# Weight chunks issued ahead of all crossbar transposes, with unit order and due times from a search

## Chip, cores, metric

The kernel runs on one core of one Trainium2 chip. The metric is the device time of one execution in microseconds (us), lower is better. In the text PE is TensorE, DVE is VectorE, ACT is ScalarE, POOL is GpSimd and SP is SyncE, as the profile calls them; "L456" is line 456 of the kernel of that run, so the same statement has different line numbers in different kernels.

## The reference

Attention with hard routing, then an MLP with exact gelu. Shapes: q, k, v are (4, 8, 768, 64), so 32 heads; 16 centroids per head; the MLP takes 3072 tokens from 512 to 2048 and back to 512.

```python
q_assign = np.argmax(np.einsum('bhsd,hcd->bhsc', q_n, c_n), axis=-1)   # q_n, k_n, c_n: normalized
k_assign = np.argmax(np.einsum('bhsd,hcd->bhsc', k_n, c_n), axis=-1)
mask = q_assign[:, :, :, None] == k_assign[:, :, None, :]
scores = np.where(mask, scale * np.matmul(q, k.transpose(0, 1, 3, 2)), -1000000000.0)
attn = softmax(scores)                       # [...] written out in the reference
x = (attn @ v).transpose(0, 2, 1, 3).reshape(B * S, H * D)
h = x @ w_in
out = (0.5 * h * (1.0 + erf(h / np.sqrt(2)))) @ w_out
```

## The kernel before

The kernel is written as a list of operations (`Op`), each with an engine, an estimated duration, dependences, and a due time. At build time a list scheduler (`Plan.run`) plays a small timing model and fixes the order in which each engine gets its instructions: it takes for each engine the operation that can start first, and among those that can start together the one with the smallest due time. The chip then runs that order, and waits where the model was wrong. A dependence that is added to this list by hand only changes the order: the chip gets no wait for it.

```python
    def run(self):
        # [...]
                    key = (t, op.due)              # t: earliest start in the model
                    if first is None or key < first:
                        first, pick = key, op
        # [...]
            dur = op.dur
        # [...]
            if op.dma:
                q = "POOL" if e == "POOL" else "SP"
                other = "SP" if q == "POOL" else "POOL"
                at = max(dma_free[q], t + 0.8)
                dma_free[q] = at + op.dma * (1.8 if dma_free[other] > at else 1.0)
                op.end = max(t + dur, dma_free[q] + 1.6) + (0.8 if t > 6 else 0.0)
```

One head goes through these steps. SP loads k, q, v (192 KB each). POOL splits k and q into a high and a low fp16 half, tile `st` (for the first three heads ACT makes the high halves). The halves are transposed into `kqT`: on PE for heads 0 to 7, by a crossbar transpose on SP for heads 8 to 31. PE then multiplies with the centroids (`asn_ps`), DVE makes one-hot rows, and these are appended to `kqT` so that the score matmul applies the mask. ACT takes the exponential of the scores (`p_sb`), PE multiplies with v (`x_ps`), DVE normalizes (`x_tok`). When 8 heads are done, PE turns the tokens (`fin_ps`, copied to `xt`) and the MLP of that batch starts: `hp`, gelu, then the second product `op`, done with seven half-size products in place of eight, for which DVE forms 16 sums of weight blocks once.

```python
            def dtr():
                nc.sync.dma_start_transpose(
                    out=new_T().rearrange("p a n d -> p (a n) d"),
                    in_=T["st", i].rearrange("p a n d -> p (a n) d"))   # heads 8 to 31
            e = add("SP", 1.4, due - 10, dtr, [sp["k"], sp["q"]], take=[s_T], dma=2.2, name=f"dtr{i}")

    def weight(n, due, deps=()):                 # 8 chunks, cast to fp16 on the way, issued by POOL
        # [...]
        w_ops[n] = add("POOL", 0.8, due,
                       lambda: nc.gpsimd.dma_start(out=dst, in_=src), deps, dma=3.6, name=f"w{n}")

    W_AT = (2, 3, 4, 5, 7, 8, 9, 10)
    # [...]
    for n in range(8):
        weight(n, need[n + 3] - 16, [splits[W_AT[n]]["k"]])   # chunk n after the split of head W_AT[n]

    def make_weight_sums(due):                   # 16 sums on DVE, 128x512 fp16 each
        for n in range(4):
            fs = slice(2 * n, 2 * n + 2)
            wd = [w_ops[4 + n // 2], w_ops[6 + n // 2]]
            o3 = add("DVE", 0.33, due, lambda fs=fs: sub(t3[:, fs], b22[:, fs], b12[:, fs]), wd, name=f"t3_{n}")
            # [...] t1, t2, t4 likewise

    # order of work: u = half a head of attention, f = half a batch of the first MLP product
    seq = [("u", *u) for u in ((0, 0), (0, 1), (1, 0), (1, 1), (2, 0), (3, 0), (2, 1), (4, 0), (5, 0), (3, 1),
        (6, 0), (7, 0), (4, 1), (5, 1))]
    seq += [("f", 0), ("u", 6, 1), ("u", 7, 1), ("u", 8, 0), ("u", 8, 1), ("f", 1)]
    # [...]
```

The softmax here doesn't subtract the row's maximum and nothing guards it: scores larger than these inputs give would overflow.

Of the kernel before, what the change touches and what calls it, by code (L numbers as in the profile page):

```python
# [15 lines left out]
BIG = 30.0  # L16

LATENCY = {"PE": 0.22, "ACT": 0.12, "DVE": 0.12, "POOL": 0.15, "SP": 0.1}

# [10 lines left out]
class Slot:  # L30


    def __init__(self, pool):
        self.pool, self.users, self.place = pool, [], None


class Plan:



    def __init__(self, pools, filler, filler_until):
        self.ops, self.pools = [], pools
        self.taken = {p: [] for p in pools}
        self.filler, self.filler_until = filler, filler_until

    def add(self, *a, **k):
        op = Op(*a, **k)
        self.ops.append(op)
        return op

    def free_at(self, slot):

        taken, bufs = self.taken[slot.pool], self.pools[slot.pool]
        if len(taken) < bufs:
            return 0.0
        last = 0.0
        for u in taken[len(taken) - bufs].users:
            if u.end is None:
                return None
            last = max(last, u.end)  # L60
        return last

    def run(self):
# [11 lines left out]
        while n:  # L75
# [35 lines left out]
            op.start = t  # L111
            dur = op.dur
            if op.func is not None and op.func != func:
# [11 lines left out]
            for s in op.take:  # L125
                self.taken[s.pool].append(s)
            done.append(op)
# [10 lines left out]
def kernel(  # L138
# [40 lines left out]
    for n in ("sc", "m", "x", "opX", "opY"):  # L179
# [25 lines left out]

    plan = Plan(POOLS, lambda: nc.tensor.matmul(warm_ps[:, 0:QB], dm[:, 0:128],
                                                dm[:, 128:128 + QB],
# [4 lines left out]
    def copy(eng, o, i):  # L212
# [5 lines left out]

    seq = [("u", *u) for u in (
        (0, 0), (0, 1), (1, 0), (1, 1), (2, 0), (3, 0), (2, 1), (4, 0), (5, 0), (3, 1),  # L220
        (6, 0), (7, 0), (4, 1), (5, 1))]
    seq += [("f", 0), ("u", 6, 1), ("u", 7, 1), ("u", 8, 0), ("u", 8, 1), ("f", 1)]
    for i in range(9, NH):
        if i % H == 1:
            seq += [("u", i, 0), ("f", 2 * (i // H) - 2), ("f", 2 * (i // H) - 1),
                    ("u", i, 1)] if i > H + 1 else [("u", i, 0), ("u", i, 1)]
        else:
            seq += [("u", i, 0), ("u", i, 1)]
    seq += [("f", 2 * B - 2), ("f", 2 * B - 1)]
    pos, at = {}, 0  # L230
# [32 lines left out]
    def memsets3():  # L263
# [10 lines left out]
        accum_out=cent_ssq), [ld_cent], name="ssq")  # L274
    c3 = add("POOL", 0.25, -79, lambda: nc.gpsimd.tensor_tensor(
        cent_norm, cent_ssq, half, op=ALU.pow), [c1, o_dm], name="root")
# [40 lines left out]
    OH_DMA = 8  # L317
    W_AT = (2, 3, 4, 5, 7, 8, 9, 10)
    ACC = set(range(0, 8))
# [4 lines left out]
    def make_load(i):  # L324
# [14 lines left out]
        loads[i] = dict(zip("kqv", ops))  # L339
        return slots  # L340

    def make_split(i, slots):
# [7 lines left out]
        for n, w in enumerate("kq"):  # L350
            def hi(w=w, n=n):
                if ("st", i) not in T:
                    T["st", i] = pool["st"].tile([128, 2, N, 2 * D], FP16, tag="st",
                                                 name="st")
                t = T[w + "st", i] = T["st", i][:, n]
                copy(eng_hi[w], t[:, :, 0:D], T[w + "raw", i])

            def lo(w=w):
                t = T[w + "st", i]
                engine[eng_lo[w]].tensor_sub(t[:, :, D:2 * D], T[w + "raw", i],  # L360
                                             t[:, :, 0:D])
            a = add(eng_hi[w], DUR[eng_hi[w]][0], due + n, hi, [ld[w]]
                    + ([hi_k] if w == "q" else []), take=[s_st] if w == "k" else [],
                    name=f"hi{w}{i}")
            hi_k = a
            c = add(eng_lo[w], DUR[eng_lo[w]][1], due + n + 0.5, lo, [a],
                    name=f"lo{w}{i}")
            res[w] = c
            slots["qkv".index(w)].users = [a, c]
        s_va = Slot("va")  # L370

        def vcast():
            nc.gpsimd.tensor_copy(vaugs[i % POOLS["va"]][:, :, 0:D], T["vraw", i])  # L373
        vc = add("POOL", 0.52, first[i] - (4 if i == 0 else 12), vcast, [ld["v"], o_va],
# [4 lines left out]

    early_ohs = {}  # L380

    def make_prep(i):
# [46 lines left out]
        else:  # L429
            def dtr():  # L430
# [4 lines left out]
                    name=f"dtr{i}")  # L435
            sp["st"].users = [e]
            ready["k"] = ready["q"] = e
        s_m = Slot("m")
# [52 lines left out]
        def ge():  # L491
            o = oh_solo[i] if solo else ohs[(i // 2) % POOLS["oh"]][:, :, i % 2]
            nc.vector.tensor_tensor(o[:, :, :, 0:C], src(),
                                    T["amax", i].to_broadcast([128, N, 2, C]),
                                    op=ALU.is_ge)
        d = 0.36 if acc else 0.28
        m1 = add("DVE", d, due + 5, amax, deps, take=[s_am], name=f"amax{i}")
        m2 = add("DVE", d, due + 5.2, ge, [m1, o_oz],
                 take=[s_oh] if s_oh is not None and i % 2 == 0 else [], name=f"ge{i}")
        if acc:  # L500
# [13 lines left out]
    def make_oh(heads):  # L514
# [7 lines left out]
        def oh(j):  # L522
            if solo:
                return oh_solo[i0][:, j].rearrange("p a b -> p (a b)")
            return ohs[(i0 // 2) % POOLS["oh"]][:, j].rearrange("p a b c -> p (a b c)")

# [7 lines left out]
        def ohdma():  # L534
            t = pool["ohT"].tile([128, N, 128], FP16, tag="ohT", name="ohT")
            nc.sync.dma_start_transpose(
                out=t, in_=ohs[(i0 // 2) % POOLS["oh"]].rearrange("p n a b c -> p (n a b c)"))
            T["ohps", i0] = t.rearrange("p n d -> p (n d)")
# [9 lines left out]
        for e, i in enumerate(heads):  # L548
# [15 lines left out]
            d = [tr, *asn_ops]  # L564
            dur = 0.35 if by_dma else 0.56
            pk = add(eng, dur if eng == "DVE" else 0.8, need[i] - 3,
# [15 lines left out]
    for n in range(8):  # L582
        weight(n, need[n + 3] - 16, [splits[W_AT[n]]["k"]])

# [4 lines left out]
    xtok_slot = {b: Slot("xtok") for b in range(B)}  # L589
    fin_ops, fin_seen = {}, set()  # L590

# [3 lines left out]
    def make_unit(i, t):  # L595
# [41 lines left out]
        for jj in range(NJ):  # L637
            def av(jj=jj):
# [5 lines left out]
                for ch in range(N):  # L644
                    nc.tensor.matmul(o, T["p", i, t][:, ch, jj * 128:(jj + 1) * 128],  # L645
                                     vaugs[i % POOLS["va"]][:, ch, 0:D + 1],
                                     start=(ch == 0), stop=(ch == N - 1))
# [19 lines left out]
        def nrm():  # L667
            if ("xtok", b) not in T:
# [5 lines left out]
                T["rec", key].to_broadcast([128, nn, D]), op=ALU.mult)  # L674
        r = add("DVE", 0.19, p0 + 5.5, rec, src, take=[Slot("rec")], name=f"rec{key}")
        m = add("DVE", 0.56 if nn == N else 0.36, p0 + 5.6, nrm, [r],
                take=[xtok_slot[b]] if ("n", b) not in norm_ops else [],
                name=f"norm{key}")
        r.take[0].users = [m]
# [10 lines left out]
    def make_fin(b, m, t, due):  # L690
        tt = (t,) if b == 0 else (0, 1)
        deps = [norm_ops[b * H + 2 * m, t], norm_ops[b * H + 2 * m + 1, t]]
        take = [] if b in fin_seen else [xt_slot[b]]
        fin_seen.add(b)
        js = slice(NJ * t, NJ * (t + 1)) if b == 0 else slice(0, N)
# [18 lines left out]
        def fin():  # L714
# [6 lines left out]
        e = add("DVE", 0.36 if nj < N else 0.56, due + 0.3, lambda: nc.vector.tensor_copy(  # L721
            xt(), T["fin", b, m, t][:, 0:nj * 128]), [f], take=take, name=f"fev{b}{m}{t}")
        s_m.users = [e]
# [58 lines left out]
    def make_weight_sums(due):  # L782
        for n in range(4):
            fs = slice(2 * n, 2 * n + 2)
            wd = [w_ops[4 + n // 2], w_ops[6 + n // 2]]
            o3 = add("DVE", 0.33, due, lambda fs=fs: sub(t3[:, fs], b22[:, fs], b12[:, fs]),
                     wd, name=f"t3_{n}")
            o1 = add("DVE", 0.33, due, lambda fs=fs: sub(t1[:, fs], b12[:, fs], b11[:, fs]),
                     [o3], name=f"t1_{n}")
            o2 = add("DVE", 0.33, due, lambda fs=fs: sub(t2[:, fs], b22[:, fs], t1[:, fs]),  # L790
                     [o1], name=f"t2_{n}")
            o4 = add("DVE", 0.33, due, lambda fs=fs: sub(t4n[:, fs], b21[:, fs], t2[:, fs]),
                     [o2], name=f"t4_{n}")
# [3 lines left out]
    def make_fc2(b, lo, hi):  # L797
# [6 lines left out]
        for n in range(NB // 2):  # L804
# [3 lines left out]
            def sums(k_, fs=fs):  # L808
# [7 lines left out]
                else:  # L816
                    sub(*{2: (s2, s1, a11), 3: (a21, a11, a21), 4: (a12, a12, s2)}[k_])
            ga, gb = gel_a[2 * n:2 * n + 2], gel_b[2 * n:2 * n + 2]
            o1 = add("DVE", 0.48, due, lambda f=sums: f(1), gb,
                     take=[s_S] if n == 0 else [], name=f"S1_{b}{n}")  # L820
            o2 = add("DVE", 0.48, due, lambda f=sums: f(2), [o1, *ga], name=f"S2_{b}{n}")
            o3 = add("DVE", 0.48, due, lambda f=sums: f(3), [o1, *ga], name=f"S3_{b}{n}")
            o4 = add("DVE", 0.48, lo + 0.46 * (hi - lo), lambda f=sums: f(4), [o2],
                     name=f"S4_{b}{n}")
# [27 lines left out]

        def result(name, j, emit, deps, due, eng="DVE", keep=None, bank=None, dur=0.36):
            take = []
# [20 lines left out]
        for k_, (p, j, xy) in enumerate(turns):  # L875
# [65 lines left out]
            if ("u3", j) in sums_out and ("p5", j) in sums_out and \  # L941
# [3 lines left out]
                    [sums_out["u3", j], sums_out["p5", j]], due + step, eng="POOL",  # L945
                    keep="o", dur=0.65)
                slots["u3", j].users.append(o)
# [50 lines left out]
```

## Time and profile before

The kernel before took 319.6 us (median of 3, 318.75 to 321.26). In the profiled execution, by engine busy time:

| | PE | ACT | DVE | POOL |
|---|---|---|---|---|
| busy, us of 319.0 | 292.8 | 217.6 | 182.5 | 118.6 |

PE is the bottleneck on average (a busy PE need not be at its peak: its matmuls overlap, so that six `hp` matmuls of 0.33 us take 1.14 us together). The average hides a hole. The next lines are from the page's view of the span in 40 slices of 8 us; a digit is tenths of the slice that PE was busy, and tenths of full clock that PE was granted:

```profile
PE   6899951799998998999999999999999999899995
PEclk9999995789999999999999999999999999999999
```

Read the sixth slice on (40 to 64 us): PE is at 5, 1 and 7 tenths, and the clock at 5 and 7 tenths follows right behind. The waits of PE, summed by what it waited for (total, times, longest, in us), name the cause:

```profile
PE asn_ps L456 <- DMA kqT<-st: 11.3, 2, 9.4
PE sc_ps L608 <- DVE kqT L560: 1.8, 4, 0.7
```

Two waits for a crossbar transpose cost 11.3 us; nothing else is over 2 us. Busy time by stretch (window, length, then busy us and instructions of each engine, then the clock, the mean number the page calls DMA share, and GB/s):

```profile
core 0: us, PE busy (x) PEld busy (x) DVE busy (x) ACT busy (x) POOL busy (x), PEclk, DMA share, GB/s
30.00:40.00 10.00, 9.53 (x180) 7.37 (x178) 8.39 (x23) 9.10 (x13) 9.75 (x16) 1.00 1.13 266
45.50:54.80 9.30, 0.00 (x0) 0.00 (x0) 0.54 (x2) 0.83 (x2) 0.00 (x0) 0.70 1.34 146
54.80:65.00 10.20, 8.21 (x87) 5.31 (x88) 4.91 (x12) 5.93 (x7) 5.54 (x9) 0.67 1.23 201
```

From 45.5 to 54.8 us PE does nothing and the other engines nearly nothing: the whole core waits for a transfer. Then PE works at about two thirds of its clock for 10 us. The transfers in question, first the two transposes by their SP instructions, then the four chunks of `w_out` by their POOL instructions (durations are min/median/max in ns):

```profile
L431 SPq DMA_TRANSPOSE kqT<-st x2: 7188/8985/10782, 36.1 to 44.6; - x2
...
  PE asn_ps L456: 11.3, 2
DMA to landing us min/median/max: 17.8/18.3/18.7
...
L312 POOL DMA_DIRECT2D w_out_sb<-in_moe_w_out_dram x4: 747/778/787, 29.0 to 41.5; - x4
DMA to landing us min/median/max: 11.9/18.7/20.7
```

The transposes of heads 8 and 9, issued at 36.1 and 44.6 us, take 18.7 and 17.8 us to land, and SP itself is held 7.2 and 10.8 us by issuing them (median of all 24: 1.6). All 24 transposes have a median of 4.7 us to land. Three weight chunks, issued at 36.2, 37.0 and 41.5 us, are in flight at the same time and take 18 to 21 us.

### The profile page before, as it was taken

Reading aid. Unit: us, or ns where it says so; the run is one execution under the profiler, and the core shown is the slowest. Engines: PE = TensorE matmul, PEld = TensorE weight load, DVE = VectorE, ACT = ScalarE, POOL = GpSimd, SP = SyncE. Lnnn points to the kernel's source line nnn. Section 1 sums busy time; section 2 is a strip of 40 time slices with the busy share of each in tenths; the row PEclk is TensorE's granted clock in tenths of the full one; section 3 lists DMA queues with packets and bytes.
Section 4 is the critical chain, followed back from the end, with each engine's and each line's share of the span. In section 5 each row is a group of like instructions: output and inputs, shape, how many; then the busy total and the mean of one; then the engine's idle time right before and its main releaser. Section 6 shows DMA issues by size and latency. Waiting matters only on the chain.

```text
span 319.0 us, 8302 instructions
## 1 busy us (share of the span) xinstructions
PE 292.8 (92%) x3392; PEld 213.9 (67%) x3392; DVE 182.5 (57%) x432; ACT 217.6 (68%) x278; POOL 118.6 (37%) x192
## 2 busy tenths in 40 slices
PE   6899951799998998999999999999999999899995
PEld 3587730467765886766667887876678887666784
DVE  4578840499689559475155558574364573203663
ACT  5487970747967887798668888896678878566200
POOL 5999921473462365566200574640000010000020
PEclk9999995789999999999999999999999999999999
DMA  7899999995982899999403799871006132100112
GB/s 265 263 246 254 257 89 162 182 243 164 174 218 65 125 194 197 253 224 238 109 0 73 176 227 181 133 153 30 2 0 111 56 78 61 51 2 0 35 66 99
DMA packets 78038, 43.50 MB, mean 136 GB/s; under 512 B 57008, under 2 KB 77488, under 8 KB 78000
## 3 DMA queue, kind: packets, MB, share of 16 engines
q1 hardware_dynamic: 75024, 38.55, 56.9%
q0 software_dynamic: 2688, 4.19, 8.5%
q8 instruction: 26, 0.43, 0.5%
q10 hardware_dynamic: 288, 0.23, 0.2%
q14 instruction: 12, 0.10, 0.1%
HBM read 27.30 MB, written 6.29 MB: 105 GB/s over the span
## 4 chain that ended last, share of the span: by engine, by line
PE 74%; DMA 12%; DVE 6%; POOL 3%; issue 2%; ACT 2%; SPq 0%; POOLq 0%; DVEq 0%
PE hp L747 26%; PE op L889 20%; PE sc_ps L608 14%; DMA kqT<-st 10%; PE x_ps L645 9%; PE asn_ps L456 2%; DVE kqT L557 2%; POOL st L360 1%; ACT p_sb L617 1%; DMA ohT<-oh 1%; PE tr_ps L412 1%; DMA v_raw<-in_v_dram 1%; DVE kqT L560 1%; DVE S L815 1%; POOL st L216 1%
## 5 line engine op out<-in xcount | busy, mean ns | idle before, releaser
L617 ACT ACTIVATE p_sb<-sc_ps 128x768 f16<-128x768 f32 x192 | 147.8, 809 | 36.9 <-PE sc_ps L608 34.5
L608 PE MATMUL sc_ps<-kqT 80*128 80x384 f16 x384 | 94.5, 329 | 2.3 <-DVE kqT L560 1.8
L747 PE MATMUL hp<-xt,w_in_sb 128*128 128x384 f16 x512 | 88.0, 329 | 0.3 <-DVE xt L721 0.2
L761 ACT ACTIVATE g<-hp 128x768 f16<-128x768 f32 x64 | 51.8, 810 | 36.3 <-PE hp L747 36.3
L747 PEld LDWEIGHTS <-w_in_sb 128*128 128x128 f16 x512 | 49.5, 99 | 32.6 <-issue 2.2
L645 PEld LDWEIGHTS <-p_sb 128*128 128x128 f16 x1152 | 57.4, 98 | 20.6 <-PE sc_ps L608 1.9
L645 PE MATMUL x_ps<-vaug,p_sb 128*128 128x65 f16 x1152 | 64.7, 195 | 1.8 <-DVE x_tok L672 1.1
L889 PEld LDWEIGHTS <-g 128*128 128x128 f16 x480 | 44.9, 97 | 10.4 <-issue 1.0
L943 POOL TENSOR_TENSOR c<-u,p 128x256 f32<-128x256 f32 x12 | 9.2, 768 | 114.5 <-DVE p L927 80.9
L889 PE MATMUL op<-w_out_sb,g 128*128 128x256 f16 x288 | 38.9, 272 | 0.2 <-DVE p L910 0.2
L608 PEld LDWEIGHTS <-kqT 80*128 80x128 f16 x384 | 29.7, 99 | 6.6 <-DVE kqT L560 2.6
L373 POOL CAST vaug<-v_raw 128x384 f16<-128x384 f32 x32 | 16.9, 530 | 43.1 <-PE x_ps L645 41.2
L360 POOL TENSOR_TENSOR st<-k_raw,st 128x384 f16<-128x384 f32 x31 | 28.7, 926 | 2.6 <-ACT st L214 0.4
L360 POOL TENSOR_TENSOR st<-q_raw,st 128x384 f16<-128x384 f32 x31 | 28.3, 919 | 1.7
L815 DVE TENSOR_TENSOR S<-g 128x768 f16<-128x768 f16 x16 | 9.5, 594 | 31.7 <-ACT g L761 31.6
L216 POOL CAST st<-k_raw 128x384 f16<-128x384 f32 x29 | 15.0, 520 | 33.6 <-DMA kqT<-st 33.6
L889 PE MATMUL op<-w_st,g 128*128 128x256 f16 x192 | 27.1, 272 | 0.4 <-DVE u L922 0.3
L472 DVE TENSOR_REDUCE asb<-asn_ps 128x192 f32<-128x384 f32 x24 | 13.3, 553 | 17.6 <-PE asn_ps L456 17.3
L456 PE MATMUL asn_ps<-c_cat,kqT 128*128 128x32 f16 x288 | 11.4, 177 | 11.3 <-DMA kqT<-st 11.3
L889 PEld LDWEIGHTS <-S 128*128 128x128 f16 x192 | 17.9, 97 | 5.5 <-DVE S L779 1.8
L672 DVE TENSOR_TENSOR x_tok<-x_ps,rec 128x384 f16<-128x384 f32 (+1 forms) x40 | 19.1, 477 | 1.3
L456 PEld LDWEIGHTS <-kqT 128*128 128x128 f16 x288 | 10.4, 96 | 13.5 <-DMA kqT<-st 11.8
(81 smaller groups left out, 276.5 us busy)
## 6 DMA issues: line engine op xcount, KB each, us to landing
q_raw<-in_q_dram SPq DMA_DIRECT2D x32, 192.0 KB, 3.4
v_raw<-in_v_dram SPq DMA_DIRECT2D x32, 192.0 KB, 4.0
out_dram<-c SPq DMA_DIRECT2D x48, 128.0 KB, 2.0
k_raw<-in_k_dram SPq DMA_DIRECT2D x31, 192.0 KB, 3.5
w_in_sb<-in_moe_w_in_dram POOLq DMA_DIRECT2D x4, 512.0 KB, 7.7
w_out_sb<-in_moe_w_out_dram POOLq DMA_DIRECT2D x4, 512.0 KB, 18.7
kqT<-st SPq DMA_TRANSPOSE x24, 4.7
k_raw<-in_k_dram ACTq DMA_DIRECT2D x1, 192.0 KB, 3.6
```

Of the source, the lines that this page charges most:

```text
L216: engine[eng].tensor_copy(o, i)
L360: engine[eng_lo[w]].tensor_sub(t[:, :, D:2 * D], T[w + "raw", i], t[:, :, 0:D])
L373: nc.gpsimd.tensor_copy(vaugs[i % POOLS["va"]][:, :, 0:D], T["vraw", i])
L456: nc.tensor.matmul(o, t[:, js], c_cat[:, h].rearrange("p a c -> p (a c)"), start=True, stop=True)
L472: nc.vector.tensor_reduce(out=T["asb", i], in_=T["asn", i].rearrange("p n w (a c) -> p n w c a", a=2), axis=AX.X, op=ALU.add)
L608: nc.tensor.matmul(s_ps[:, e, 0:QB], T["kT", i][0:D + C, c * 128:(c + 1) * 128], T["qT", i][0:D + C, t * QB:(t + 1) * QB], start=True, sto ...
L617: nc.scalar.activation(T["p", i, t][:, 2 * cp:2 * cp + 2, :], T["sc", i, t, cp][:, :, 0:QB], ACT_FN.Exp, bias=0.0, scale=float(scale))
L645: nc.tensor.matmul(o, T["p", i, t][:, ch, jj * 128:(jj + 1) * 128], vaugs[i % POOLS["va"]][:, ch, 0:D + 1], start=(ch == 0), stop=(ch == N ...
L672: nc.vector.tensor_tensor(T["xtok", b][:, h // 2, j0:j0 + nn, h % 2 * D:(h % 2 + 1) * D], T["x", key][:, :, 0:D], T["rec", key].to_broadca ...
L747: nc.tensor.matmul(T["hp", hb, fp][:, e, 0:QB], w_in_sb[:, m, f * 128:(f + 1) * 128], T["xt", b][:, m, t * QB:(t + 1) * QB], start=(m == 0 ...
L761: nc.scalar.activation(T["g", hb][:, :, fp, :], T["hp", hb, fp][:, :, 0:QB], ACT_FN.Gelu, bias=0.0, scale=1.0)
L889: nc.tensor.matmul(T["op", b, key], a()[:, f, j * 128:(j + 1) * 128], w[:, f, :], start=(start and f == 0), stop=(f == NB - 1), skip_group ...
```

## The change

The intent: issue the weight chunks earlier, so that all of them have landed before the first crossbar transpose; hold the splits and transposes of heads 8 and later behind the last chunk in the plan; correct the durations of the timing model; and search, on that model, over the order of the units and over a shift of the due time of single operations. No arithmetic is added or removed. Buffers that were picked by head number are picked in the order of emission, so that the new order stays correct.

```diff
+ORDER = ("0a 0b 1a 1b 2a 3a 4a 5a 2b 6a 7a 4b 5b 3b f0 6b 7b 8a 8b f1 9a 9b [...] f6 f7 ")
+SHIFT = dict(... "fc2_2_P6_0_1=41 fc2_0_P1_1_1=20 [... about 1,600 entries ...] av14a1=-5")
     def add(self, *a, **k):
         op = Op(*a, **k)
+        op.due += self.shift.get(op.name, 0)
-            dur = op.dur
+            dur = op.dur + (0.03 if e == "DVE" else 0.0)
-    W_AT = (2, 3, 4, 5, 7, 8, 9, 10)
+    W_AT = (1, 2, 3, 4, 5, 6, 7, 7)
-        weight(n, need[n + 3] - 16, [splits[W_AT[n]]["k"]])
+        weight(n, need[W_AT[n]] - 14, [splits[W_AT[n]]["kq"[n == 7]]])
+    for i in range(8, NH):
+        if i not in PE_TR:
+            first_hi[i].deps.append(w_ops[7])      # first split of head i
+            dtrs[i].deps.append(w_ops[7])          # its crossbar transpose
-            o3 = add("DVE", 0.33, due, ...         # the 16 weight sums
+            o3 = add("DVE", 0.69, due, ...
-                nc.gpsimd.tensor_copy(vaugs[i % POOLS["va"]][:, :, 0:D], T["vraw", i])
+                nc.gpsimd.tensor_copy(vaugs[turn("va", i)][:, :, 0:D], T["vraw", i])
[... other durations (S sums 0.48 to 0.58, results 0.36 to 0.41), the same for the one-hot buffers ...]
```

`ORDER` is nearly the old order: half a head is moved here and there. Most of the search's result is in `SHIFT`.

The two dependences on `w_ops[7]` are called the explicit waits below.

## The prediction

> **What bounds it now.** TensorE: 292.8 of 319.0 us busy. But busy is not peak: from the trace's start-to-start times (0.16 us per 384-column matmul, 0.11 per 256, 0.03 per 65) I estimate only about 250 us of matmul work. In stretches (busy time by window), the lost time sits in three places:
> - 45.5 to 54.8 us: TensorE does nothing. The waits view gives 9.4 us to the first crossbar transpose of an attention head (kqT from st, head 8), and 2.0 us to the next, ending at 62.5. Both together are 10% of the chain of waits. The granted clock is 0.50 from 50 to 58 and 0.60 from 62 to 66, which I estimate at 3 us more. [...]
> - 100 to 147 us: TensorE 43.3 of 47 us, ScalarE 39.7. Neither is saturated; the chain goes through a one-hot transpose (4.2 us), a kqT transpose (5.4), POOL splits.
> - 147 to 213.6: 66.6 us for one steady batch; the next batch takes 62.7. ScalarE's own work there (48 exps, 16 gelus paced by TensorE, 2 table loads) is about 61.
>
> **Why the transposes stall.** The first transposes start at 36.1 and 44.6 us and take 18.7 and 17.8 us to land (median of all 24: 4.7). Three weight chunks, issued by POOL at 36.2, 37.0 and 41.5, are in flight and take 18 to 21 us (the first ones took 7 to 10). SP is itself held 7.2 and 10.8 us by the two transpose issues (1.3 to 1.6 normally), and POOL idles 12.6 us for a st buffer. [...]
>
> **What changes.** No arithmetic is added or removed. Instruction order shows weights issued earlier in POOL's stream, and heads 8 and later split and transposed only after the last chunk has landed. Adding up POOL's durations, the last three chunks move from 36.2/37.0/41.5 to about 31/32/33 us. 38 loads plus all weights are 11.7 MB; at the 257 GB/s of the first 32 us that lands near 45 us. Then POOL splits (4.7 us) and the transpose (about 4.5) make head 8 ready near 54. In the new order its assignment matmul stands about 38 gelu-stage matmuls into the first MLP half, which TensorE should reach at 57 to 60 us: no stall.
>
> **Sum (estimates).**
> - Stall and half clock gone; the first MLP half starts near 51.5 instead of 62.8: -11 to -13 us.
> - 100 to 147: heads no longer late, order re-searched with truer VectorE durations: -2 to -6.
> - Steady batches: -1 to -4. Tail (fc2 work pulled before the last transposes): -1.
> - Possible losses: loads slowed by denser weights early, a short wait for one-hots of heads 8/9: +1 to +4.
>
> Predicted 300 us (before 319.6), 8-in-10 range 292 to 308. Faster by over 2%: 0.94; within 2%: 0.05; slower: 0.01.
>
> **What would show it.** Right: no TensorE wait over 2 us on kqT from st; kqT landings 4 to 6 us with no 18 us outliers; clock 1.00 from 16 us on; first gelu at 51 to 55 us (before 65.9); last weight landing at 43 to 48 us; batch period 62 to 65 us; TensorE busy below 290.
>
> **What would make it wrong.** Chunks landing after 50 us, so the stall returns at head 8 behind the explicit wait; early raw loads starved, so the first exps come later; transposes slow for another reason than weights (loads alone); or the 100 to 147 loss being a real ScalarE/TensorE balance, which leaves only the first term (about 307).

## The result, and the profile after

The changed kernel took 302.41 us (median of 4, 301.71 to 303.06), against 320.13 us (4 runs, 318.75 to 321.26) for the kernel before in the same comparison. A run of a kernel counts as slow when it is over 1.5% above the fastest of the same kernel. A ratio here is always the mean time of one kernel's fast runs over that of the other's fast runs of the same rounds, so it is not quite the ratio of the medians: 0.9448, 95% interval 0.94 to 0.9496. It is faster by 5.5%.

The same slices of the page, now of the changed kernel (301.1 us, so 7.5 us each):

```profile
PE   7899878999989999999999999999999999999995
PEclk9999999999999999999999999999999999999999
```

The hole and the dip of the clock are gone. The longest entries of PE's waits:

```profile
PE sc_ps L844 <- ACT p_sb L853: 2.8, 7, 0.6
PE sc_ps L844 <- DVE kqT L791: 1.6, 3, 0.7
PE warm_ps L436 <- DVE half L465: 1.5, 1, 1.5
```

No wait for a crossbar transpose is left in the whole list; the longest single wait, 1.5 us, is at the start of the program. The same stretches (columns as before) and the transfers:

```profile
30.00:40.00 10.00, 8.85 (x173) 7.06 (x169) 8.47 (x23) 7.04 (x11) 4.35 (x7) 1.00 1.15 286
45.50:54.80 9.30, 8.28 (x103) 5.36 (x101) 9.03 (x19) 9.20 (x13) 8.82 (x11) 1.00 0.66 158
54.80:65.00 10.20, 10.20 (x110) 6.83 (x107) 7.25 (x16) 5.78 (x8) 7.68 (x12) 1.00 1.07 203
```

```profile
L661 SPq DMA_TRANSPOSE kqT<-st x3: 1278/1525/1986, 49.5 to 56.6; - x3
...
DMA to landing us min/median/max: 3.8/4.4/6.2
...
L533 POOL DMA_DIRECT2D w_out_sb<-in_moe_w_out_dram x4: 740/761/787, 21.7 to 33.5; - x4
DMA to landing us min/median/max: 9.3/12.0/12.2
```

The last chunk is issued at 33.5 and lands 12.2 us later, at 45.7. POOL pauses (4.35 of 10 us busy in 30 to 40, the wait for PE named above), then does the splits of heads 8 and later at full load. The first transposes start at 49.5 us and land in 3.8 to 6.2 us. Note that DVE, ACT and POOL are all above 8.8 of 9.3 us busy in the stretch where they had stood still.

Where did the 17.9 us of the span go? ACT loads its gelu table when it comes to each MLP stage, which gives the same marker in each kernel: at 61.42, 87.86, 147.31, 214.17 and 273.64 us before, at 52.60, 75.62, 130.76, 197.71 and 254.38 us after. The stretches between them, first before, then after:

```profile
61.42:87.86 26.44, 25.18 (x258) 17.29 (x259) 21.25 (x46) 18.27 (x23) 13.70 (x20) 0.94 0.95 200
87.86:147.31 59.45, 55.70 (x716) 41.26 (x716) 41.61 (x92) 48.18 (x62) 31.86 (x48) 1.00 0.90 182
147.31:214.17 66.86, 66.73 (x772) 49.49 (x771) 37.32 (x92) 52.61 (x67) 26.84 (x41) 1.00 0.68 139
214.17:273.64 59.47, 59.47 (x645) 44.24 (x643) 29.98 (x73) 45.58 (x57) 2.34 (x3) 1.00 0.25 55
```

```profile
52.60:75.62 23.02, 22.82 (x258) 16.42 (x257) 16.99 (x38) 17.95 (x22) 16.30 (x25) 1.00 1.01 194
75.62:130.76 55.14, 53.98 (x716) 40.80 (x714) 40.01 (x92) 48.11 (x61) 29.39 (x44) 1.00 0.92 197
130.76:197.71 66.95, 66.60 (x784) 49.67 (x783) 42.11 (x95) 52.56 (x66) 30.64 (x46) 1.00 0.73 154
197.71:254.38 56.67, 56.67 (x609) 41.68 (x608) 28.79 (x70) 45.19 (x58) 2.28 (x3) 1.00 0.27 57
```

| stretch | before | after | difference |
|---|---|---|---|
| start to first MLP stage | 61.42 | 52.60 | -8.8 |
| first to second | 26.44 | 23.02 | -3.4 |
| second to third | 59.45 | 55.14 | -4.3 |
| third to fourth (a batch with 16 attention units) | 66.86 | 66.95 | +0.1 |
| fourth to fifth (a batch with 13 units) | 59.47 | 56.67 | -2.8 |
| fifth to end | 45.36 | 46.72 | +1.4 |

In the first two of these four stretches the matmul counts are equal in both kernels (258 and 716), so a shorter stretch there is lost time recovered. But 2.2 of the 3.4 us between the first two markers only make up for the first row: the table load stood 1.4 us before the first matmul of its stage in the kernel before, and 0.8 us after it in the changed one. In the fourth stretch the counts differ: it has 36 matmuls fewer, which now stand in the tail after the fifth marker. So those two rows belong together: -1.4 us.

### The profile page after: what moved, and what is told of

It reads as the page before. It is cut to its first block, busy times and chain, and to the rows that moved or that the text cites. A ratio compares the mean times of both kernels' runs of the same rounds, so it can differ in the third digit from the quotient of the medians.

```text
span 301.1 us, 8247 instructions
## 1 busy us (share of the span) xinstructions
PE 287.6 (96%) x3388; PEld 212.5 (71%) x3388; DVE 186.4 (62%) x432; ACT 216.3 (72%) x278; POOL 120.6 (40%) x192
## 4 chain that ended last, share of the span: by engine, by line
PE 81%; DVE 10%; ACT 5%; issue 1%; DMA 1%; POOL 0%; ACTq 0%; DVEq 0%
PE hp L983 25%; PE op L1125 22%; PE sc_ps L844 17%; PE x_ps L881 10%; ACT p_sb L853 5%; PE asn_ps L687 2%; DVE g L1015 2%; DVE kqT L791 2%; DVE kqT L788 1%; PE tr_ps L642 1%; DMA cent_sb<-in_centroids_dram 1%; PE both_ps L642 1%; DVE S L1015 1%; DVE S L1051 1%; PE warm_ps L436 1%
## 5 line engine op out<-in xcount | busy, mean ns | idle before, releaser
L844 PE MATMUL sc_ps<-kqT 80*128 80x384 f16 x384 | 92.3, 325 | 4.6 <-ACT p_sb L853 2.8
L983 PE MATMUL hp<-xt,w_in_sb 128*128 128x384 f16 x512 | 85.9, 326 | 0.0
L997 ACT ACTIVATE g<-hp 128x768 f16<-128x768 f32 x64 | 51.8, 811 | 35.4 <-PE hp L983 35.2
L881 PEld LDWEIGHTS <-p_sb 128*128 128x128 f16 x1152 | 47.7, 97 | 12.8 <-PE sc_ps L844 1.5
L881 PE MATMUL x_ps<-vaug,p_sb 128*128 128x65 f16 x1152 | 52.0, 193 | 1.1 <-DVE x_tok L908 1.1
L844 PEld LDWEIGHTS <-kqT 80*128 80x128 f16 x384 | 32.1, 98 | 11.7 <-issue 4.8
L583 POOL TENSOR_TENSOR st<-q_raw,st 128x384 f16<-128x384 f32 x31 | 29.1, 943 | 1.7
L703 DVE TENSOR_REDUCE asb<-asn_ps 128x192 f32<-128x384 f32 x24 | 13.3, 555 | 13.1 <-PE asn_ps L687 12.9
L908 DVE TENSOR_TENSOR x_tok<-x_ps,rec 128x384 f16<-128x384 f32 (+1 forms) x40 | 19.1, 477 | 1.3
L901 DVE RECIPROCAL rec<-x_ps 128x6 f32<-128x6 f32 (+1 forms) x40 | 7.5, 186 | 16.7 <-PE x_ps L881 16.2
L446 POOL CAST st<-q_raw 128x384 f16<-128x384 f32 x29 | 16.3, 564 | 3.1 <-DMA q_raw<-in_q_dram 3.1
```

The costliest lines, as they stand in the source:

```text
L446: engine[eng].tensor_copy(o, i)
L583: engine[eng_lo[w]].tensor_sub(t[:, :, D:2 * D], T[w + "raw", i], t[:, :, 0:D])
L703: nc.vector.tensor_reduce(out=T["asb", i], in_=T["asn", i].rearrange("p n w (a c) -> p n w c a", a=2), axis=AX.X, op=ALU.add)
L844: nc.tensor.matmul(s_ps[:, e, 0:QB], T["kT", i][0:D + C, c * 128:(c + 1) * 128], T["qT", i][0:D + C, t * QB:(t + 1) * QB], start=True, sto ...
L881: nc.tensor.matmul(o, T["p", i, t][:, ch, jj * 128:(jj + 1) * 128], vaugs[turn("va", i)][:, ch, 0:D + 1], start=(ch == 0), stop=(ch == N - 1))
L908: nc.vector.tensor_tensor(T["xtok", b][:, h // 2, j0:j0 + nn, h % 2 * D:(h % 2 + 1) * D], T["x", key][:, :, 0:D], T["rec", key].to_broadca ...
```

## The experiments

Two explanations fit the result. One: the order of the weight chunks carries it, because it removes the transfer stall. Two: the search carries it, and the chunks matter little. All kernels below gave correct results. Where an expectation names theories by letters, they are the rivals of that experiment, and the paragraph after it says in words what held. Line numbers differ by kernel. The medians are of all runs, slow ones too; the ratios are of fast runs alone. One run of the kernel before, of 1028.94 us, counts as slow and is left out.

| experiment | median us | ratio to before | 95% interval |
|---|---|---|---|
| weights only | 318.43 | 0.9997 | 0.9929 to 1.0064 |
| search only | 315.02 | 0.9876 | 0.9825 to 0.9928 |
| everything but the shifts | 314.2 | 0.9838 | 0.977 to 0.9906 |
| everything but the explicit waits | 310.64 | 0.972 | 0.9662 to 0.9778 |
| the same, started warm | 307.76 | 0.9574 | 0.9524 to 0.9624 |
| before, clock kept up | 319.68 | 0.997 | 0.9913 to 1.0027 |
| before, late chunks after two transposes | 318.45 | 0.9969 | 0.9886 to 1.0052 |
| before, assignment matmuls later | 316.67 | 0.995 | 0.9874 to 1.0026 |
| weights only, sums later | 315.46 | 0.9855 | 0.9798 to 0.9912 |
| weights only, sums spread | 312.09 | 0.9747 | 0.9706 to 0.9788 |
| no shifts, sums spread | 310.5 | 0.9738 | 0.967 to 0.9806 |
| after, started warm | 302.14 | 0.9436 | 0.9401 to 0.9471 |
| (the change) | 302.41 | 0.9448 | 0.94 to 0.9496 |

### Weights only

The kernel before, with the new chunk order and the explicit waits, and nothing else.

```diff
-    W_AT = (2, 3, 4, 5, 7, 8, 9, 10)
+    W_AT = (1, 2, 3, 4, 5, 6, 7, 7)
-        weight(n, need[n + 3] - 16, [splits[W_AT[n]]["k"]])
+        weight(n, need[W_AT[n]] - 14, [splits[W_AT[n]]["kq"[n == 7]]])
+    for i in range(8, NH):
+        if i not in PE_TR:
+            first_hi[i].deps.append(w_ops[7])
+            dtrs[i].deps.append(w_ops[7])
```

> The kernel before with one part of the change: weight chunks placed earlier, and heads 8 and later split and transposed only after the last chunk landed. No searched order, old durations in the plan. Theory W (weight chunks in flight make the first crossbar transposes slow, and TensorE stands behind them): transposes of heads 8 and 9 land in 4 to 6 us, TensorE waits under 2 us for kqT, clock 1.00 after 16 us, time 306 to 310 us. Rival O (the gain is in the searched order): 315 to 320 us.

Measured: 318.43 us, no gain: the time that rival O named, with the mechanism that theory W named. The stall is gone: the transposes are issued at 51.4 and 54.2 us and each lands in 4.0 us, and no wait for `kqT` by transfer is left. PE's waits, and the stretches where the hole had been, in this kernel:

```profile
PE x_ps L655 <- DVE x_tok L682: 3.5, 4, 2.1
PE fin_ps L727 <- DVE x_tok L682: 3.3, 3, 2.2
```

```profile
45.00:50.00 5.00, 2.54 (x30) 1.32 (x28) 4.97 (x11) 4.00 (x6) 5.00 (x8) 1.00 0.42 106
50.00:55.00 5.00, 1.95 (x29) 1.36 (x30) 4.93 (x11) 1.51 (x2) 4.84 (x6) 0.69 0.70 152
55.00:60.00 5.00, 5.00 (x41) 3.03 (x39) 2.55 (x7) 3.31 (x4) 1.06 (x2) 0.62 0.93 228
```

PE is again under half busy from 45 to 55 us, and again drops its clock, but now it waits for DVE, which is full. What fills DVE is its timeline from 46 to 52 us (start, duration of the group, count at the end of the line):

```profile
46.09 1.75 DVE L789 TENSOR_TENSOR w_out_sb<-w_out_sb 128x512 f16<-128x512 f16 x2
47.77 1.13 DVE L789 TENSOR_TENSOR w_st<-w_out_sb 128x512 f16<-128x512 f16 x1
...
50.58 1.71 DVE L789 TENSOR_TENSOR w_st<-w_out_sb 128x512 f16<-128x512 f16 x2
```

These are the weight sums. The first of them need the last chunk but one, which lands at 44.5 us (the last lands at 47.2); from 44.6 to 57.6 us all 16 run nearly back to back, ahead of the normalizations that PE waits for. The model had them at 0.33 us each; here one takes 0.41 to 1.13 us. So the transfer order does what was intended, and the time it frees is eaten by work that it releases. In the changed kernel the sums run in the same stretch, 44.1 to 58.9 us, and one takes 0.41 to 1.13 us there too, but more of the other DVE work stands between them.

### Search only

The changed kernel with the old chunk order and without the explicit waits.

```diff
-    W_AT = (1, 2, 3, 4, 5, 6, 7, 7)
+    W_AT = (2, 3, 4, 5, 7, 8, 9, 10)
-        weight(n, need[W_AT[n]] - 14, [splits[W_AT[n]]["kq"[n == 7]]])
+        weight(n, need[n + 3] - 16, [splits[W_AT[n]]["k"]])
-            first_hi[i].deps.append(w_ops[7])
-            dtrs[i].deps.append(w_ops[7])
```

> The changed kernel with the weight chunks back at the old places and without the waits for the last chunk; searched order, due times and plan durations kept. Theory W: landings of about 18 us for the first two transposes return, TensorE waits 6 to 10 us for kqT, clock falls to 0.5, time 312 to 317 us. Rival O: 301 to 305 us.

Measured: 315.02 us, as theory W expected. The stall is there, as the first of PE's waits shows:

```profile
PE asn_ps L687 <- DMA kqT<-st: 8.1, 2, 7.7
```

The transpose of head 8 is issued at 39.2 us among chunks issued at 38.6, 39.9 and 43.4 us, and takes 13.3 us. Alone the halves measured 0.0% and 1.2%; together they give 5.5%. The parts are not additive: each leaves a wait in place that the other removes. The search had been made with the early chunks in place; what a new search with the old chunk order would reach was not tried.

### Late chunks after two transposes

Does the transpose suffer from the weight chunks, or from the raw loads that are always in flight? Here, in the kernel before, the last three chunks are ordered behind the transposes of heads 8 and 9.

```diff
+    for n in (5, 6, 7):
+        w_ops[n].deps += [dtrs[8], dtrs[9]]
```

> The kernel before, but the last three weight chunks are issued only after the transposes of heads 8 and 9 have landed. Theory W: these two transposes land in 4 to 6 us although raw loads are in flight, no TensorE wait over 2 us at head 8; the chunks then slow a transpose of heads 10 to 13 instead, so 306 to 316 us. Rival L (raw loads alone slow the transposes): landings stay over 10 us and the time stays near 319.

The landing times in this kernel: the two transposes without the last three chunks beside them, the next one beside the chunks, and those chunks.

```profile
L433 SPq DMA_TRANSPOSE kqT<-st x2: 1890/2872/3853, 37.1 to 42.2; - x2
DMA to landing us min/median/max: 5.9/6.5/7.1
...
L433 SPq DMA_TRANSPOSE kqT<-st x1: 6052/6052/6052, 48.4 to 48.4; - x1
DMA to landing us min/median/max: 15.2/15.2/15.2
...
L312 POOL DMA_DIRECT2D w_out_sb<-in_moe_w_out_dram x3: 750/762/790, 47.1 to 48.6; - x3
DMA to landing us min/median/max: 8.7/11.9/14.5
```

The slow landing went with the chunks to the next transpose, and so did the stall (PE waits 11.5 us for `kqT`, 9.5 at most, at 55 to 63 us); the time stayed, 318.45 us, above the 306 to 316 that theory W expected. The cleanest of these landings is head 9's, 5.9 us with only raw loads in flight for all but its last 1 us; beside head 8's (7.1 us) the first chunk of `w_out`, issued at 29.1, was in flight until about 41 us (an estimate: the same chunk took 11.9 us in the kernel before). Over all runs with the chunks placed differently, the landing of head 8's transpose goes with what is in flight:

| run | weight chunks beside the transpose | landing, us |
|---|---|---|
| before; assignment later; clock kept up | three, issued from 2.3 us before to 5.5 us after it | 18.7; 19.1; 18.0 |
| search only | three, issued from 0.5 us before to 4.3 us after it | 13.3 |
| no explicit waits, started warm | two, which land about 3 and 7 us after its issue | 10.2 |
| no explicit waits | two, which land about 2 and 4 us after its issue | 5.7 |
| late chunks (heads 8 and 9) | none of the last three | 7.1, 5.9 |
| weights only; no shifts; sums spread | none | 4.0; 4.6; 4.1 |

That the transposes are slow beside the chunks, and not beside raw loads alone, is shown. How (which queue or which engine gives way) no run shows. Nor does any run show that transposes alone give way, for plain loads slow down as well: in the kernel before, the loads issued from 32.2 to 35.4 us took 9.1 to 9.9 us (medians of all are 3.4 to 4.0).

The same run gives the other missing number. Its weight sums run at 70 to 79 us, when POOL is idle. The timeline of DVE and a stretch of it:

```profile
70.82 0.75 DVE L784 TENSOR_TENSOR w_out_sb<-w_out_sb 128x512 f16<-128x512 f16 x2
```

```profile
70.80:72.90 2.10, 2.10 (x15) 1.26 (x14) 2.10 (x7) 1.60 (x2) 0.00 (x0) 1.00 0.37 94
```

Here a pair takes 0.75 us, with POOL at 0.00 (one sum 0.41 us, by the median of the run). In "weights only", a pair of the same shape takes 1.71 to 1.75 us, with POOL busy with splits for all of 46.1 to 52.3 us (6.20 of 6.20). In the same run the last three sums, from 56.0 to 57.6 us, take 0.41 to 0.42 us each, where POOL is busy for only 0.50 of the 2 us from 56 to 58. So the slow sums stand beside splits, though not every sum beside splits is slow (0.45 us at 49.08); what makes them slow no run shows.

### Assignment matmuls later

Can PE's order alone hide the stall? In the kernel before, the two assignment matmuls that wait are tied behind pieces of the first MLP stage.

```diff
+    by_name["asnk8"].deps.append(by_name["fc1_0_4_3"])
+    by_name["asnk9"].deps.append(by_name["fc1_0_7_3"])
```

> The kernel before, weights untouched; only the assignment matmuls of heads 8 and 9 are moved behind the first 20 and 32 matmul pieces of the first MLP half in TensorE's order. Landings stay near 18 us in any theory. If slow landings hurt only because TensorE's queue stands behind them (rival O): the wait for kqT goes, about 307 us. If they also hold back POOL (12.6 us idle for a st buffer) and make the later heads late (theory W): at most half is won, 311 to 316 us, with new waits between 75 and 130 us.

Measured: 316.67 us, not to be told from before, and closest to theory W. The first MLP stage begins at 51.37 us, 10 us earlier, and the wait for the transpose is gone although it lands in 19.1 us. But the next stretch grows from 26.4 to 28.5 us and the one after from 59.5 to 61.1. Head 8 is still late, and PE runs out of other work: from 70 to 80 us it is busy 7.07 of 10 us. Ten microseconds gained at 51 us have shrunk to about 6 us at the third MLP stage, and the timed runs show less.

### Clock kept up

Fifty-four dummy matmuls ahead of head 8's assignment in the kernel before, meant to keep PE's clock up through the stall, and so to price the half clock by itself.

```diff
+            if i == 8 and not first_asn:
+                warm = pool["opX"].tile([128, QB], FP32, tag="opX", name="warm8_ps")
+                for _ in range(54):
+                    nc.tensor.matmul(warm, dm[:, 0:128], dm[:, 128:128 + QB], start=True, stop=True)
```

> The kernel before with 54 extra matmuls (about 9 us of work, result unused) in TensorE's queue just ahead of the stalled assignment of head 8. If the halved clock after the stall costs what I estimated (about 3 us): granted clock 1.00 until 62 us, and 315.5 to 317.5 us. If TensorE is held by other waits there anyway: 318.5 to 320 us.

Inconclusive, and a miss: 319.68 us. In the profiled run the transpose was issued 2.5 us later this time and landed at 56.5; the fillers ended at 54.3, with the clock at 1.00 from 45 to 55 us (0.70 in 45.5 to 54.8 us before); and after a gap of 2.28 us it was at 0.50 until 63 us all the same. A gap of that length did not always do this: in "sums later", below, PE waits 2.3 us once for an assignment, and the mean clock of the whole run is 1.000. The runs differ, though: the mean clock was 0.989 and 0.993 in two of the four fast runs (319.63 and 319.72 us), and 0.999 and 0.998 in the other two, which took 316.47 and 318.9 us. So, as an estimate from these four times, a clock that stays up may be worth some 1 to 3 us, but two runs of each kind don't measure it. What the half clock costs is not measured separately.

### Sums later

"Weights only", with the weight sums tied behind the first MLP matmul.

```diff
+    for n in range(4):
+        by_name[f"t3_{n}"].deps.append(by_name["fc1_0_0_0"])
```

> The weights-only kernel (318.4 us), and VectorE's 16 sums over the output weights are held until the first matmul of the first MLP half. Theory S (the weights-only version lost its gain because the sums, now ready at 44 us, stand in VectorE's queue ahead of the normalisations that TensorE waits for): TensorE no longer idles at 48 to 54 us, the first gelu table load comes at 51 to 53 us instead of 58.2, time 309 to 314 us. Rival T (the gain is lost elsewhere, at each later stage): the first table load moves, but the time stays at 316 to 319 us.

Measured: 315.46 us, between the two ranges. The first stage begins at 51.79 us, but the block of sums moved as a whole: PE is busy 3.88 and 2.75 of 5 us in the two stretches from 55 to 65 us, DVE 4.97 and 4.10. One can see the hole travel: with the chunks, with the transposes, with the sums.

### Sums spread

"Weights only", with each of the 16 sums tied to its own PE step, every second one from the 36th piece of the first scores and MLP matmuls on.

```diff
+    for n in range(4):
+        for k_, t_ in enumerate(("t3", "t1", "t2", "t4")):
+            by_name[f"{t_}_{n}"].deps.append(seq_ops[35 + 2 * (4 * n + k_)])
```

> The weights-only kernel (318.4 us), with each of VectorE's 16 weight sums held until a later matmul piece of TensorE's order, so that they stand between the normalisations. Theory S (the sums in one block are what cancels the gain; held until the first MLP half they only moved the block): first gelu table load at 51 to 53 us and the second at 76 to 79 us, TensorE idle under 3 us between 45 and 70 us, time 307 to 312 us. Rival T (late heads lose it later in any case): 313 to 317 us.

Measured: 312.09 us, at the edge of theory S's range; ratio 0.9747 against 0.9997 without the spread. The first two stages begin at 51.93 and 78.49 us, and PE loses 2.3 us in 45 to 70 us where "weights only" lost 5.5. The same stretches as above, of this kernel:

```profile
45.00:50.00 5.00, 4.35 (x61) 3.00 (x62) 3.58 (x9) 4.81 (x8) 5.00 (x9) 1.00 0.50 129
50.00:55.00 5.00, 4.79 (x56) 3.15 (x53) 4.52 (x10) 4.58 (x6) 4.84 (x7) 1.00 0.79 175
```

So the placing of the sums is what kept "weights only" from paying; a hand-made rule for it brings 2.5% of the change's 5.5%.

### Everything but the shifts

The changed kernel with new order, chunks, waits and durations, but without `SHIFT`.

```diff
-        op.due += self.shift.get(op.name, 0)
```

> The changed kernel with the new unit order, new plan durations, new weight places and waits, but without the searched shifts of due times. If the corrected durations are enough to keep VectorE's sums and the heads in place: 303 to 307 us. If the shifts carry the rest: 309 to 316 us.

Measured: 314.2 us. Right durations in the model do not place the work well by themselves. The first stage begins at 56.80 us, PE waits 2.9 us for `x_tok` and its clock is 0.62 and 0.70 in 45 to 55 us. The loss against the change is spread over the span: +4.2 us to the first MLP stage, then +2.0, +1.5, +2.0 and +3.7, and -1.3 in the tail.

### No shifts, sums spread

The kernel above with the spread sums. If the shifts buy mainly the placing of the sums, this should come near the change.

```diff
-        op.due += self.shift.get(op.name, 0)
+            by_name[f"{t_}_{n}"].deps.append(seq_ops[35 + 2 * (4 * n + k_)])
```

> The changed kernel without its shifts of due times (as the run without shifts, 314.2 us), and the 16 VectorE weight sums each tied to one TensorE step of the first score and MLP pieces, as in the run that spread them in the kernel before. Theory S1 (what the searched shifts buy is mostly the placing of the weight sums): 306 to 309 us, first gelu table load near 52 to 53, TensorE idle in 45 to 70 us below 2.5 us. Rival S2 (the shifts buy many small things through the whole span; the spread repairs only the first stage): 311 to 313, first table load near 53, and the later stages as in the run without shifts (table load to table load 25, 57, 69, 60 us).

Measured: 310.5 us (fast runs 310.25 to 310.5), between the two ranges, 0.5 us below the rival's and over 1 us above the first theory's. The first stage begins at 52.52 us, as in the change (52.60), 4.3 us earlier than without the spread; that is the whole gain. About 8 us are left to the change, in the later stages (3.1 of them by the third marker, 133.81 against 130.76). (The profiled run: 315.11 us with a mean clock of 0.989, against 0.993 to 0.998 in the fast ones. Its clock is 1.00 in every stretch from 30 to 100 us; its stages after the third marker are not compared.) So the placing of the sums is worth about 4 us of what the shifts buy; what the rest consists of was not taken apart, and by the loss per stage above it is spread over the span.

### No explicit waits, and the same started warm

The changed kernel without the dependence of later heads on the last chunk.

```diff
-            first_hi[i].deps.append(w_ops[7])
-            dtrs[i].deps.append(w_ops[7])
```

> The changed kernel without the explicit waits of heads 8 and later for the last weight chunk; the chunks stay early. Theory W: the transpose of head 8 is issued at about 38 us while chunks are in flight until 45 us, so it lands in 8 to 14 us, but near 50 us, before TensorE needs it at about 52; time 301 to 306 us. If the waits themselves matter: over 308 us.

Measured: 310.64 us. But in this trace a pair of score matmuls took 0.80 to 0.83 us until about 28 us (the expectation below says 23), against 0.49 in the change, although the clock column shows 1.00 in both. The two starts agree until about 11 us (six transposes at 9.7 us take 0.85 and 0.84 us); from 11.2 us on six transposes take 0.49 us in the change, and 0.80 here. A start with slow matmuls is called cold below; what makes it so no run shows. It ends well before the first transpose that the waits concern (45.8 us here). So it was run again with two more dummy matmuls in the start-up, and the change itself was given the same two.

```diff
+        for _ in range(3 if fills[0] == 10 else 1):
+            nc.tensor.matmul(warm_ps[:, 0:QB], dm[:, 0:128], dm[:, 128:128 + QB], start=True, stop=True)
```

> The changed kernel without the waits for the last chunk, as in the run that gave 310.6 us, plus two extra filler matmuls at 4.8 us. In that run's trace the score matmuls took 0.80 us a pair until 23 us, as cold, though all other runs have 0.49 from 14 us. Theory C (a cold start cost 6 us there, the waits cost little): pairs take 0.49 from 12 us on and the time is 302 to 306 us. Rival D (the waits themselves are worth it): pairs at 0.49, but 307 to 312 us.

Measured: 307.76 us (fast runs 305.63 to 309.23, mean 306.8; two runs, the profiled one too, were slow ones). In its trace a pair of score matmuls takes 0.49 us from 12.6 us on. That is between the two theories: with the warm start the time is about 4 us lower, and about 4 us remain. Head 8's transpose goes out at 40.7 us beside the last chunks, takes 10.2 us, holds SP for 4.1, and PE waits 2.3 us. Against the warm change (0.9574 against 0.9436) the explicit waits, that is the order they lead to, are worth about 1.4%, 4 us. The search had been made with the waits in place, so a search without them could lose less.

> The changed kernel plus the same two extra filler matmuls before the centroid transpose, which close TensorE's first gap. If the clock rises earlier than 10 us: transposes of the first heads at 0.5 instead of 0.84 us per six, first score matmul about 0.5 us earlier, time 301 to 302.5 us against 302.4. If the fillers only delay the centroid chain: 302.5 to 303.5 us.

The change with two more dummy matmuls: 302.14 us, ratio 0.9436 against 0.9448, no difference to be told. Its first scores come at 12.85 in place of 13.95 us, and the span ends 0.4 us earlier. No kernel clearly beats the change.

## Why the prediction was right, and where it was not

The prediction was 300 us, 292 to 308; measured 302.41. The terms, one by one:

- **Cause of the stall: right.** It blamed the chunks in flight. The landings moved with the chunks in every run, and a transpose with raw loads alone beside it took 5.9 us. But its picture of heads that wait for the last chunk was a wait of the plan, not of the chip (POOL starts the first split of the later heads at 44.07 us, before the last chunk has landed at 45.7).
- **Chunk times: right.** Issue was estimated at 31, 32 and 33 us and came at 30.7 to 33.5; the last landing was estimated at 43 to 48 and came at 45.7. Transposes land in 3.8 to 6.2 us (4 to 6 predicted).
- **"Stall and half clock gone; the first MLP half starts near 51.5": right.** By the first matmul of that half, 62.8 became 51.8, -11.0 us (-11 to -13 predicted). The first gelu comes at 53.9 (51 to 55 predicted), the clock is 1.00 from 16 us on, PE's busy time 287.6 (below 290 predicted).
- **"100 to 147: -2 to -6": right in size.** The stretch between the second and third MLP stage, with the same PE work, fell by 4.3 us. The stretch before it gave 3.4, of which 2.2 is the place of the marker and a part the half clock. The cause it gave (heads no longer late, better order) is only partly tested: without the shifts this stretch is 56.6 us, so the shifts hold 1.5 of the 4.3.
- **"Steady batches: -1 to -4": the step that failed.** It read 66.6 us for one batch against 62.7 for the next as slack in the first, and expected a batch period of 62 to 65 us. Measured by the same markers: 66.86 became 66.95, and 59.47 became 56.67. The difference was one of work and not of slack: the order puts 16 half-head units between the markers of the first and only 13 between those of the next, and PE, 66.73 of 66.86 us busy in the first, had next to no wait left there to remove. The 2.8 us of the second are not a shorter batch either, since half of them come back in the tail (+1.4) with the work that moved there. Net, from the third marker to the end, the change gives -1.3 us (0.1 - 2.8 + 1.4), where the prediction had -2 to -5 together with its "tail -1".
- **"Possible losses +1 to +4": mostly not seen.** Loads of q land in 4.1 us (median) in place of 3.4, and no stage got longer for it.
- **Not foreseen: that the move of the chunks alone is worth nothing.** The prediction put -11 to -13 us on it and treated the search as a supplement of 3 to 10 us. The runs show that neither pays alone (0% and 1.2%). The 16 weight sums become ready when the last two chunks land, in the middle of the splits, where one takes up to 1.13 us against 0.41 beside an idle POOL. The total came out right because the search took care of that, not because the prediction saw it.

What stays open: how the chunks slow the transposes, and what makes the sums slow beside the splits; what gap lowers the clock; what the half clock costs alone; how the gain of the search divides among order, durations and shifts beyond "without shifts 314.2"; and why one kernel started cold when nearly the same start-up did not.

## What to carry to other kernels

Here one late transfer stopped the core, and the work behind it was released together; so look there for the next limit before counting a stall as gain: moving the transfers removed 11 us of waiting and 0 us of time until the DVE sums that they released were spread out. A repair of one wait moved the hole four times (to another transpose, to later heads, to DVE, to DVE later), and the marker of each later stage showed it, which the start of the repaired stage did not. Before comparing two "batches" in a trace, count the units in each.
